# Attention inside a mixture-of-experts kernel: probabilities kept as float32 stationary operands, q and k laid out by the host

## The chip, the cores and the metric

The kernel runs on one core of one Trainium2 chip. The metric is the device time of one execution in microseconds (us). The engines are named as the profile names them: PE is TensorE (matrix products; PEld is its loading of the stationary operand), DVE is VectorE, ACT is ScalarE, POOL is GpSimd, SP issues DMAs. A matrix product holds one operand in the array (stationary, loaded first) and streams the other past it (moving).

## What is computed

Three stages: attention on queries that are averaged in pairs, a dense layer pair with a softmax gate and layer norm, and eight experts of which each token takes one. Only the first stage and the host's part are touched.

```python
B, H, S, D = 4, 8, 1152, 64
q_pool = q.reshape(B, H, S // 2, 2, D).mean(axis=3)
scores = (1.0 / np.sqrt(D)) * np.matmul(q_pool, k.transpose(0, 1, 3, 2))
scores = scores - np.max(scores, axis=-1, keepdims=True)
attn = np.exp(scores)
attn = attn / (np.sum(attn, axis=-1, keepdims=True) + 1e-09)
attn_out = np.matmul(attn, v)
...
x = attn_out.transpose(0, 2, 1, 3).reshape(B * S // 2, H * D)
```

## The kernel before

`attention` (line 95) works through 32 heads of 576 pooled queries and 1152 keys. A head is cut into 9 **units**; a unit holds two of the 18 pairs (half of the queries, chunk of 128 keys). float32r is a type of which TensorE takes fewer bits than float32 has, so a float32 value is carried as two float32r parts, high and low.

- `scores` (L267): per unit four products of 288 columns into one `pair` of PSUM banks. `k1` holds high and low parts of the keys, `q1` the high part of the queries twice, and `k2`/`q2` the remaining part together with two rows that subtract the row maximum. ACT then takes the exponential of the bank twice: `ph` rounded to float32r (L281) and `e` in float32 (L282). DVE subtracts them to the low part `pl` (`rest`, L286).
- `pv` (L288): two units later, three float32r products per (half, chunk): stationary the 65 columns of `vh` or `vl` (v and a column of ones, which sums the probabilities), moving 288 columns of `ph` or `pl` (L295, L296, L297). The result is transposed, 65 rows by 288 queries. `finish`, `norm` and `scale` divide it by its sum, by way of DRAM.
- `prepass` (L241): the row maximum must be known before the exponential. For a later head, 14 products (12 of 384 columns, 2 of 288) into a ring of two `bank`s, each followed by a reduction on DVE (L255). `shift` (L259) turns the maxima into rows of `q2`.
- q, k arrive in rows; PE turns them (`transposes`, L211, 19 per head, in the free columns of a `pair`) and ACT copies the result out (`evacuate`, L218). POOL splits q, k and v into parts (L150, L154, L163).

The order of every engine is the order in which the Python code emits instructions (`manual_schedule`). It is set by a table of due times in units: head n starts at g = 9 n, and `at(g - 12.6 + 0.68 * i, prepass, n, i)` puts its part of the maximum two heads ahead. In a unit come: four score products, transposes, the two exponentials, then the products of the unit before last with events between them, then the remaining events, then `pl`. The fillers (L62 to L92) convert weights that arrive as two words. The dense layers start after the last head.

## Time and profile before

| what | us |
|---|---|
| median of three runs | 1198.6 (1197.12 to 1201.09) |
| span of the profiled execution | 1196.7 |
| first score product to last score product (32 heads) | 19.0 to 596.9 |
| the rest: dense layers and experts | 597 to 1196.7 |

The page of the profile gives the span of the profiled execution, from its first to its last instruction, and no other time of it; the three runs lie 0.4 to 4.4 us above that span, the median 1.9 us. Over the span PE is busy for 90%, DVE for 86%, ACT for 70%, POOL for 64%. These are averages over stages with different limits: heads fill the first half, dense layers and experts the second.

### The profile page before, as it was taken

The numbers are of one execution on the slowest core, as the hardware profiler recorded it, in microseconds if no ns is written. First come the engines' busy times: TensorE is split into PE (matmuls) and PEld (weight loads), VectorE is DVE, ScalarE is ACT, GpSimd is POOL, SyncE is SP. The second block draws the span as 40 slices with busy tenths as digits, with TensorE's granted clock in tenths as the row PEclk, the third lists the DMA queues.
The fourth block names the chain that finished last, engine by engine and source line by source line (L and its number), as shares of the span: only waits on it lengthen the run. The fifth ranks groups of instructions, "written<-read, shape, count | busy, mean of one in ns | idle before, by whom it ended". The sixth has DMA issues, their size and how long they took to land. (4 is left out here: it accounts for less than half of the span.)

```text
span 1196.7 us, 19933 instructions
## 1 busy us (share of the span) xinstructions
PE 1075.0 (90%) x6359; PEld 943.0 (79%) x6359; DVE 1029.4 (86%) x1604; ACT 839.4 (70%) x1637; POOL 760.3 (64%) x844
## 2 busy tenths in 40 slices
PE   7999998999999999999998999979726999999996
PEld 6889888888888888888877777767624888888885
DVE  7898888988899999999758788887999898999983
ACT  5787777877788888878844644444634788888883
POOL 7888888888888888898566676665775221111211
PEclk8999999999999999999998999998878899999998
DMA  5344334344444444443120000004352789533700
GB/s 150 94 107 128 107 106 113 101 118 113 114 114 113 123 114 116 119 114 96 54 85 19 27 18 18 18 18 168 105 176 79 233 285 335 165 114 99 258 18 19
DMA packets 73866, 133.83 MB, mean 112 GB/s; under 512 B 22044, under 2 KB 24092, under 8 KB 73632
## 3 DMA queue, kind: packets, MB, share of 16 engines
q1 hardware_dynamic: 69936, 122.79, 33.9%
q0 software_dynamic: 3680, 9.45, 2.2%
q8 instruction: 52, 0.85, 0.3%
q14 instruction: 54, 0.44, 0.1%
q10 hardware_dynamic: 144, 0.29, 0.1%
HBM read 146.02 MB, written 10.82 MB: 131 GB/s over the span
## 5 line engine op out<-in xcount | busy, mean ns | idle before, releaser
L286 DVE TENSOR_TENSOR pl<-e,ph 128x576 fp32r<-128x576 f32 x288 | 286.5, 995 | 17.5 <-ACT e L282 16.4
L255 DVE TENSOR_REDUCE m<-bank 128x1 f32<-128x384 f32 (+1 forms) x435 | 218.2, 528 | 42.7 <-PE bank L254 38.3
L272 PE MATMUL pair<-q,k 128*128 128x288 f32 x1152 | 205.6, 302 | 0.1
L281 ACT ACTIVATE ph<-pair 128x576 fp32r<-128x576 f32 x288 | 190.8, 662 | 3.0 <-PE pair L272 2.8
L282 ACT ACTIVATE e<-pair 128x576 f32<-128x576 f32 x288 | 190.9, 663 | 0.0
L272 PEld LDWEIGHTS pair<-q,k 128*128 128x128 f32 x1152 | 181.2, 193 | 0.5 <-ACT q L224 0.4
L295 PE MATMUL acc<-ph,vh 128*65 128x288 f32 x576 | 179.1, 311 | 0.0
L297 PE MATMUL acc<-pl,vh 128*65 128x288 f32 x576 | 172.5, 299 | 1.0 <-DVE pl L286 0.8
L296 PE MATMUL acc<-ph,vl 128*65 128x288 f32 x576 | 172.2, 299 | 0.0
L970 POOL DMA_INDIRECT out_y<-x,rows x23 | 25.2, 1095 | 202.0 <-ACT x L969 197.4
L254 PE MATMUL bank<-k,q 128*128 128x384 f32 (+1 forms) x435 | 140.8, 345 | 11.9 <-DVE m L255 10.6
L855 DVE SCALAR_TENSOR_TENSOR junk<-x,en 128x512 f32<-128x512 f32 x99 | 145.9, 1474 | 2.4
L756 PE MATMUL acc<-wo_hi,lh 128*128 128x512 f32 x264 | 109.2, 414 | 14.2 <-ACT lh L868 14.2
L756 PE MATMUL pair<-wi_hi,xl 128*128 128x512 f32 x268 | 106.7, 398 | 5.6 <-DVE xl L931 5.6
L756 PE MATMUL pair<-wi_hi,xh 128*128 128x512 f32 x268 | 109.0, 407 | 0.0
L756 PE MATMUL acc<-wo_hi,ll 128*128 128x512 f32 x264 | 107.1, 406 | 0.4 <-DVE ll L869 0.4
L756 PE MATMUL acc<-wo_lo,lh 128*128 128x512 f32 x264 | 106.1, 402 | 1.2 <-DVE wo_lo L781 1.2
L756 PE MATMUL pair<-wi_lo,xh 128*128 128x512 f32 x268 | 105.8, 395 | 0.0
L254 PEld LDWEIGHTS bank<-k,q 128*128 128x128 f32 (+1 forms) x435 | 79.7, 191 | 20.3 <-DVE m L255 18.8
L224 ACT CAST q<-pair 128x256 fp32r<-128x256 f32 x128 | 48.1, 376 | 60.2 <-PE pair L214 60.2
L869 DVE TENSOR_TENSOR ll<-bank,lh 128x512 fp32r<-128x512 f32 x82 | 52.7, 684 | 40.7 <-ACT lh L868 39.7
L296 PEld LDWEIGHTS acc<-ph,vl 128*65 128x65 f32 x576 | 80.4, 140 | 5.3
(216 smaller groups left out, 2653.2 us busy)
## 6 DMA issues: line engine op xcount, KB each, us to landing
raw<-in_moe_w SPq DMA_DIRECT2D x184, 512.0 KB
vn<-in_v SPq DMA_DIRECT2D x32, 288.0 KB
k<-k SPq DMA_DIRECT2D x32, 288.0 KB
kn<-in_k SPq DMA_DIRECT2D x31, 288.0 KB
k<-k SPq DMA_DIRECT2D x62, 144.0 KB
qn<-in_q SPq DMA_DIRECT2D x32, 256.0 KB
rb<-rd SPq DMA_DIRECT2D x32, 144.0 KB
xT<-xu SPq DMA_DIRECT2D x32, 144.0 KB
```

What stands on the lines that cost most here:

```text
L254: nc.tensor.matmul(out=pp[:p, :w], lhsT=lhsT, rhs=rhs[:, u * w:(u + 1) * w])
L255: nc.vector.tensor_reduce(out=m3[:p, t, u:u + 1], in_=pp[:p, :w], axis=AX.X, op=ALU.max)
L272: nc.tensor.matmul(out=ps[:, i, :QH], lhsT=d[f"k{j}"][:, ch * P:(ch + 1) * P], rhs=d[f"q{j}"][:, hf * QH:(hf + 1) * QH], start=(j == 1), s ...
L281: nc.scalar.activation(out=ph, in_=sv, func=AF.Exp, scale=SC)
L282: nc.scalar.activation(out=e, in_=sv, func=AF.Exp, scale=SC)
L286: nc.vector.tensor_tensor(out=pl, in0=e, in1=ph.bitcast(F32), op=ALU.subtract)
L295: nc.tensor.matmul(out=acc, lhsT=vh, rhs=ph[:, i], start=(ch == 0), stop=False)
L296: nc.tensor.matmul(out=acc, lhsT=d["vl"][:, ch, 0:D + 1], rhs=ph[:, i], start=False, stop=False)
L297: nc.tensor.matmul(out=acc, lhsT=vh, rhs=pl[:, i], start=False, stop=(ch == KC - 1))
L756: nc.tensor.matmul(out=out, lhsT=lhsT, rhs=rhs, start=first and id(out) not in outs[:i], stop=last and id(out) not in outs[i + 1:])
L855: nc.vector.scalar_tensor_tensor(out=self.junk("v", DM), in0=x2, scalar=1.0, in1=en, op0=ALU.mult, op1=ALU.mult, accum_out=to)
L869: nc.vector.tensor_tensor(out=hl[:, o], in0=pt, in1=hh[:, o].bitcast(F32), op=ALU.subtract)
```

## The change

- **Exponentials.** `scores` makes one exponential per unit, `e` in float32, into a ring of four buffers with 640 columns, of which the last 64 are zero. `ph`, `pl` and `rest` are gone. A unit is now one chunk of keys for all 576 queries.
- **Products with v.** `pv` has five float32 products per unit: stationary a block of 128 columns of `e`, moving the 66 columns of `v` (64, a column of ones, a column of zeros), all five into one bank. The result stands in rows of queries, so `norm` divides it on DVE straight from PSUM, without DRAM; after each second head `turned` transposes it with five products and two copies on ACT. v is loaded straight into place and no longer split.
- **q and k.** The host stores them transposed. The on-chip transposes (19 per head), their copies on ACT and `dup_q3`/`dup_k3` are gone. Two heads share the tiles `qn`, `kn`, `kl`, `qs`, one in the upper and one in the lower 64 rows. `split_q` and `split_k` write high parts with ACT, low parts with POOL (DVE for the first two heads), and DMAs copy them to the other 64 rows.
- **Row maximum.** 15 products of 384 columns per head, instead of 14. `shift` transposes on DVE and writes the rows of `q2` with four small DMAs.
- **Order of tokens.** It is now the natural one (`rows_of` is gone).

```diff
+        EARLY = ((-14.82, 0.75), (-3.97, 0.55), (4.4, 0.55))
+        vs = [sb.tile([P, KC, D + 2], F32, name=f"v{i}") for i in range(3)]
+        k2s = [sb.tile([P, S], F32R, name=f"k2{i}") for i in range(2)]
+        q1s = [sb.tile([P, QT * P], F32R, name=f"q1{i}") for i in range(4)]
+        q2s = [sb.tile([P, QT * P], F32R, name=f"q2{i}") for i in range(2)]
+        es = [sb.tile([P, QT * P], F32, name=f"e{i}") for i in range(4)]
...
         def load_q(n):
...
+            nc.sync.dma_start(out=shared(n, "qn", [P, 2, NQ])[mine(n)[0]], in_=q[b, h])
...
         def load_k(n):
...
+            (nc.sync if n else nc.scalar).dma_start(out=shared(n, "kn", [P, S])[mine(n)[0]], in_=k[b, h])
...
         def load_v(n):
...
+            st[n]["v"] = t = vs[n % 3]
+            nc.sync.dma_start(out=t[:, :, 0:D], in_=v[b, h].rearrange("(c p) d -> p c d", p=P))
...
         def split_q(n):
...
+            r, o = mine(n)
+            qn, qs = shared(n, "qn", [P, 2, NQ]), shared(n, "qs", [P, NQ], bufs=2)
+            st[n]["q1"] = q1 = q1s[n % 4][:, 0:NQ]
+            (nc.gpsimd if n > 1 else nc.vector).tensor_tensor(out=qs[r], in0=qn[r, 0], in1=qn[r, 1], op=ALU.add)
+            nc.scalar.copy(out=q1[r], in_=qs[r])
+            nc.sync.dma_start(out=q1[o].bitcast(F32), in_=q1[r].bitcast(F32))
...
         def split_q2(n):
...
+            r, o = mine(n)
+            st[n]["q2"] = q2 = q2s[n % 2]
+            nc.gpsimd.tensor_tensor(out=q2[r, 0:NQ], in0=shared(n, "qs", [P, NQ])[r], in1=st[n]["q1"][r].bitcast(F32),
+                                    op=ALU.subtract)
...
         def split_k(n):
...
+            r, o = mine(n)
+            kn, kl = shared(n, "kn", [P, S]), shared(n, "kl", [P, S], F32R)
+            st[n]["k1"] = k1 = sb.tile([P, S], F32R, tag="k1", name="k1", bufs=4)
+            nc.scalar.copy(out=k1[r], in_=kn[r])
+            (nc.gpsimd if n > 1 else nc.vector).tensor_tensor(out=kl[r], in0=kn[r], in1=k1[r].bitcast(F32),
+                                                              op=ALU.subtract)
+            nc.sync.dma_start(out=k1[o].bitcast(F32), in_=kl[r].bitcast(F32))
...
         def dup_k(n):
...
+            r, o = mine(n)
+            st[n]["k2"] = k2 = k2s[n % 2]
+            nc.sync.dma_start(out=k2[r].bitcast(F32), in_=st[n]["k1"][r].bitcast(F32))
...
         def prepass(n, i):
...
+            u, t = divmod(i, QT)
+            w = S // 3
             pp = c.acc() if n < 2 and i % 2 else c.bank()
...
+            nc.tensor.matmul(out=pp[:, :w], lhsT=q1s[n % 4][:, block(t)], rhs=st[n]["k1"][:, u * w:(u + 1) * w])
+            nc.vector.tensor_reduce(out=m3s[n % 2][:, t, u:u + 1], in_=pp[:, :w], axis=AX.X, op=ALU.max)
...
         def shift(n):
...
             nc.vector.tensor_reduce(out=nm, in_=m3s[n % 2], axis=AX.X, op=ALU.max, negate=True)
-            t = d["q2n"]
-            high(t[:, :, 0], nm)
-            low(t[:, :, 1], nm, t[:, :, 0])
...
+            nc.vector.tensor_copy(out=t[:, 0:QT], in_=nm)
+            nc.vector.tensor_tensor(out=t[:, QT:2 * QT], in0=nm, in1=t[:, 0:QT].bitcast(F32), op=ALU.subtract)
+            nc.vector.transpose(out=nt, in_=t.bitcast(F32))
+            row = D - n % 2 * D
+            dst = st[n]["q2"][row:row + 2].bitcast(F32).rearrange("a (t x) -> a t x", x=P)
+            for x in range(0, P, 32):
+                nc.sync.dma_start(out=dst[:, :, x:x + 32], in_=nt[x:x + 2 * QT])
...
+        def scores(n, ch):
             d = st[n]
             ps = c.pair()
-            for i, (hf, ch) in enumerate(items):
+            for hf in range(2):
                 for j in (1, 2):
-                    nc.tensor.matmul(out=ps[:, i, :QH], lhsT=d[f"k{j}"][:, ch * P:(ch + 1) * P],
+                    nc.tensor.matmul(out=ps[:, hf, :QH], lhsT=d[f"k{j}"][:, ch * P:(ch + 1) * P],
                                      rhs=d[f"q{j}"][:, hf * QH:(hf + 1) * QH], start=(j == 1), stop=(j == 2))
...
-            ph = sb.tile([P, 2, QH], F32R, tag="ph", name="ph", bufs=3)
-            pl = sb.tile([P, 2, QH], F32R, tag="pl", name="pl", bufs=3)
...
-            sv = ps[:, :, :QH]
-            nc.scalar.activation(out=ph, in_=sv, func=AF.Exp, scale=SC)
-            nc.scalar.activation(out=e, in_=sv, func=AF.Exp, scale=SC)
-            return ph, pl, e
...
-        def rest(ph, pl, e):
-            nc.vector.tensor_tensor(out=pl, in0=e, in1=ph.bitcast(F32), op=ALU.subtract)
...
-        def pv(n, items, ph, pl, i):
+            e = es[(n * KC + ch) % 4]
+            nc.scalar.activation(out=e[:, 0:NQ].rearrange("p (a b) -> p a b", a=2), in_=ps[:, :, :QH], func=AF.Exp, scale=SC)
+            return e
...
+        def pv(n, ch, e, t):
...
-                vh = d["vh"][:, ch, 0:D + 1]
-                nc.tensor.matmul(out=acc, lhsT=vh, rhs=ph[:, i], start=(ch == 0), stop=False)
-                nc.tensor.matmul(out=acc, lhsT=d["vl"][:, ch, 0:D + 1], rhs=ph[:, i], start=False, stop=False)
-                nc.tensor.matmul(out=acc, lhsT=vh, rhs=pl[:, i], start=False, stop=(ch == KC - 1))
...
+            if ch == t == 0:
+                d["acc"] = c.acc()[:, 0:QT * (D + 2)].rearrange("p (t x) -> p t x", t=QT)
+            nc.tensor.matmul(out=d["acc"][:, t], lhsT=e[:, block(t)], rhs=d["v"][:, ch],
+                             start=(ch == 0 and t == 0), stop=(ch == KC - 1 and t == QT - 1), skip_group_check=True)
...
         def norm(n):
+            acc, d = st[n]["acc"], st[n - n % 2]
+            rz = xn.tile([P, QT], F32, tag="rz", name="rz", bufs=2)
+            nc.vector.tensor_scalar(out=rz, in0=acc[:, :, D], scalar1=EPS, scalar2=None, op0=ALU.add)
+            nc.vector.reciprocal(out=rz, in_=rz)
+            if n % 2 == 0:
+                d["xq"] = xn.tile([P, QT, P], F32, tag="xq", name="xq", bufs=2)
+            nc.vector.tensor_tensor(out=d["xq"][:, :, mine(n)[0]], in0=acc[:, :, 0:D],
+                                    in1=rz[:, :, None].to_broadcast([P, QT, D]), op=ALU.mult)
+        def turned(n):
...
+            xq = st[n - 1]["xq"]
+            xu = xn.tile([P, NQ], F32, tag="xu", name="xu", bufs=2)
+            for lo, hi in ((0, QT - 1), (QT - 1, QT)):
+                pt = c.bank().rearrange("p (a b) -> p a b", b=P)
+                for t in range(lo, hi):
+                    nc.tensor.transpose(pt[:, t - lo], xq[:, t], c.idf)
+                if lo == 0:
+                    nc.scalar.copy(out=xu[:, 0:4 * P].rearrange("p (a b) -> p a b", b=P), in_=pt)
+                else:
+                    nc.scalar.copy(out=xu[:, 4 * P:], in_=pt[:, 0, 0:D])
+            nc.sync.dma_start(out=xT[:, h // 2, b * NQ:(b + 1) * NQ].bitcast(F32), in_=xu)
             st[n].clear()
...
+            at(g - 31, load_k, n)
+            at(g - 30.5, load_q, n)
+            at(g - 15, load_v, n)
+            at(g - 26, split_q, n)
+            at(g - 25, split_k, n)
+            at(g - 8, split_q2, n)
+            at(g - 8.5, dup_k, n)
+            for i in range(3 * QT):
+                at(EARLY[n][0] + EARLY[n][1] * i if n < 3 else g - 13.2 + 0.6 * i, prepass, n, i)
+            at(g - 3.6, shift, n)
             for i, f in enumerate(filler(n)):
                 at(g + (-3, 1, 2, 3)[i], f)
...
+            at(g + 11, norm, n)
+            if n % 2:
+                at(g + 12.5, turned, n)
...
-                time = n * NU + u
-                job = jobs.get(time)
-                ph, pl, e = scores(n, items, job and job[0](*job[1:]))
...
+            for ch in range(KC):
+                e = scores(n, ch)
+                todo = due(n * KC + ch + 1)
...
-                for i in range(2):
-                    if todo:
+                for t in range(QT):
+                    if todo and t in (0, 2):
                         todo.pop(0)()
                     if old:
-                        pv(*old, i)
+                        pv(*old, t)
...
-        for blk in range(2 * NTT):
-            base, step = rows_of(blk)
-            r = (blk % 2) * D
-            iota(None, None, [[0, 1]], base=base + 1, mult=step, out=row[r:r + D, blk // 2:blk // 2 + 1])
+        iota(None, None, [[P, NTT]], base=1, mult=1, out=row)
...
-        a = np.ascontiguousarray(inputs[name])
+        a = np.asarray(inputs[name])
+        if name == "q":
+            a = a.reshape(B, H, NQ, 2, D).transpose(0, 1, 4, 3, 2)
+        elif name == "k":
+            a = a.transpose(0, 1, 3, 2)
+        a = np.ascontiguousarray(a)
         if a.dtype == np.float64:
```

PE, about half way through the heads. Before: one unit. `q`, `k` are the score operands, `idr`/`khl` a transpose, `ph`, `pl`, `vh`, `vl` the products with v, `bank` the row maximum.

```order
L272 MATMUL pair<-q_4119,k_4185 128x288
L272 MATMUL pair<-q_4641,k_130 128x288
L272 MATMUL pair<-q_4119,k_4185 128x288
L272 MATMUL pair<-q_4641,k_130 128x288
L214 MATMUL pair<-idr,khl 128x128 x2
L295 MATMUL acc<-ph,vh_126 65x288
L296 MATMUL acc<-ph,vl_135 65x288
L297 MATMUL acc<-pl,vh_126 65x288
L254 MATMUL bank<-k_4476,q_4410 128x384
L295 MATMUL acc<-ph,vh_126 65x288
L296 MATMUL acc<-ph,vl_135 65x288
L297 MATMUL acc<-pl,vh_126 65x288
```

PE in the changed kernel, one unit at about the same place; `v`, `e` are the float32 products.

```order
L214 MATMUL pair<-q_134,k_2697 128x288
L214 MATMUL pair<-q_136,k_130 128x288
L214 MATMUL pair<-q_134,k_2697 128x288
L214 MATMUL pair<-q_136,k_130 128x288
L192 MATMUL bank<-k_2900,q_131 128x384
L224 MATMUL acc<-v_126,e_138 128x66 x2
L192 MATMUL bank<-k_3087,q_132 128x384
L224 MATMUL acc<-v_126,e_138 128x66 x3
```

The scores and the row maximum stand as before; six products of 288 columns and two transposes became five of 66 columns.

DVE, before: about three units. `m` is a part of the row maximum, `pl` the low part, `raw` a filler, `dc` the sums of the probabilities.

```order
L286 TENSOR_TENSOR pl<-e,ph 128x576
L67 TENSOR_SCALAR a<-raw 128x256
L69 SCALAR_TENSOR_TENSOR a<-raw,a 128x256
L71 TENSOR_SCALAR m<-raw 128x256
L255 TENSOR_REDUCE m_133<-bank 128x1 x2
L286 TENSOR_TENSOR pl<-e,ph 128x576
L255 TENSOR_REDUCE m_133<-bank 128x1
L286 TENSOR_TENSOR pl<-e,ph 128x576
```

DVE in the changed kernel: most of one head. `rz`, `xq` are the division, `nm`, `nt` the rows that subtract the maximum.

```order
L193 TENSOR_REDUCE m_142<-bank 128x1 x2
L230 TENSOR_SCALAR rz<-acc 128x5
L231 RECIPROCAL rz<-rz 128x5
L234 TENSOR_TENSOR xq<-acc,rz 128x5x64
L193 TENSOR_REDUCE m_142<-bank 128x1 x4
L193 TENSOR_REDUCE m_141<-bank 128x1 x2
L200 TENSOR_REDUCE nm<-m_142 128x5
L201 CAST nm_144<-nm 128x5
L202 TENSOR_TENSOR nm_144<-nm,nm_144 128x5
L203 STREAM_TRANSPOSE nt<-nm_144 128x32
L193 TENSOR_REDUCE m_141<-bank 128x1 x7
L67 TENSOR_SCALAR a<-raw 128x256
```

The subtraction in every unit is gone; the reductions of the maximum stay, and six short instructions per head (division and rows of the maximum) take the place of two (L313, L314).

## Rows read from the trace of the kernel before

**Rows 1.** Busy time by stretch: us, then each engine's busy us (instructions), PE clock.

```profile
300.00:480.70 180.70, 169.43 (x1243) 159.27 (x1242) 168.89 (x292) 146.17 (x333) 156.04 (x193) 0.99 0.42 117
```

**Rows 2.** Instructions by line, 300 to 480.7 us, DVE and ACT: busy us, mean ns | idle.

```profile
L286 DVE TENSOR_TENSOR pl<-e,ph 128x576 fp32r<-128x576 f32 x91 | 95.6, 1050 | 2.8 <-ACT e L282 2.7
L255 DVE TENSOR_REDUCE m<-bank 128x1 f32<-128x384 f32 x121 | 62.3, 541 | 7.3 <-PE bank L254 6.5
L281 ACT ACTIVATE ph<-pair 128x576 fp32r<-128x576 f32 x91 | 60.3, 662 | 0.0
L69 DVE SCALAR_TENSOR_TENSOR a<-raw,a 128x256 int32<-128x256 int32 x10 | 4.3, 425 | 0.3
L79 ACT ACTIVATE s<-raw 128x256 f32<-128x256 int32 x10 | 4.5, 453 | 0.0
L313 DVE TENSOR_SCALAR dc<-dc 64x9 f32<-64x9 f32 x10 | 5.6, 559 | 1.3 <-DMA dc<-xu 1.3
```

**Rows 3.** Waits, 300 to 480.7 us: us in total, times, longest.

```profile
PEld bank L254 <- DVE m L255: 7.6, 11, 0.9
PE pair L214 <- POOL q2n L154: 6.6, 7, 2.0
```

**Rows 4.** PE in order of time, about two units: start us, length us.

```profile
300.64 0.70 PE L272 MATMUL pair<-q,k 128*128 128x288 f32 x4
301.18 0.28 PE L214 MATMUL pair<-idr,q1n 128*128 128x128 f32 x2
301.30 0.31 PE L295 MATMUL acc<-ph,vh 128*65 128x288 f32 x1
...
302.11 0.34 PE L254 MATMUL bank<-k,q 128*128 128x384 f32 x1
302.28 0.69 PE L272 MATMUL pair<-q,k 128*128 128x288 f32 x4
```

**Rows 5.** Short products with 128 stationary columns, in order of time.

```profile
829.66 1.42 PEld L699 LDWEIGHTS bank<-bb,xT 128*128 128x128 f32 x12 [2.42 <-DVE ll L869]
829.66 1.51 PE L699 MATMUL bank<-bb,xT 128*128 128x20 f32 x12 [1.99 <-DVE ll L869]
...
760.55 1.03 PE L866 MATMUL bank<-idf,ln 128*128 128x128 f32 x8
```

**Rows 6.** One line's instructions: ns min/median/max, first and last start us.

```profile
L699 PEld LDWEIGHTS bank<-bb,xT x12: 186/192/193, 829.7 to 830.9; 128*128 128x128 f32 x12
L866 PE MATMUL bank<-idf,ln x328: 270/272/475, 613.1 to 1178.3; 128*128 128x128 f32 x164
L866 PEld LDWEIGHTS bank<-idf,ln x328: 137/140/230, 613.1 to 1178.2; 128*128 128x128 f32 x164
L214 PEld LDWEIGHTS pair<-idr,khl x288: 137/140/223, 6.9 to 564.4; 128*128 128x128 f32 x144
L272 PE MATMUL pair<-q,k x1152: 289/296/445, 19.0 to 596.9; 128*128 128x288 f32 x192
```

**Rows 7.** Instructions by line, 300 to 480.7 us, POOL.

```profile
L323 POOL TENSOR_TENSOR xu<-xu,rb 64x576 f32<-64x576 f32 x10 | 18.9, 1893 | 0.0
L154 POOL TENSOR_TENSOR khl<-kn,khl 128x576 fp32r<-128x576 f32 x10 | 15.0, 1499 | 0.8
L87 POOL TENSOR_TENSOR z<-a,z 128x256 f32<-128x256 f32 x10 | 11.9, 1192 | 0.8
L81 POOL TENSOR_SCALAR z<-m 128x256 f32<-128x256 int32 x10 | 8.5, 847 | 16.9 <-DVE m L71 16.9
```

**Rows 8.** Start of the program, and SP's issues of one line, in order of time.

```profile
0.80 0.41 SPq L131 DMA_DIRECT2D qn<-in_q  x1
...
4.80 0.55 DVE L163 TENSOR_TENSOR qs<-qn 128x256 f32<-128x256 f32 x2 [1.76 <-DMA qn<-in_q]
...
8.46 0.69 PE L254 MATMUL bank<-k,q 128*128 128x384 f32 x1 [0.46 <-ACT k L224]
...
307.96 0.55 SPq L257 DMA_DIRECT2D m<-m  x1
```

252 lines of the change are left out of this document (41 added, 211 removed).

## The prediction, made before the run

> **What bounds the kernel now.** I read the heads first, since nothing else changes. From the first to the last score product they take 596.9 - 19.0 = 577.9 us [rows 6], 18.06 us for each of 32 heads. What ends a head? Busy time by stretch [rows 1] has PE at 169.4 and DVE at 168.9 of 180.7 us over ten heads, but the two mean different things. A PE product counts with its pipeline, so the true pace must come from the starts in order of time [rows 4]: four scores from 300.64 to 301.18 are 0.135 us each, six products with v from 301.30 to 302.11 also 0.135, one part of the row maximum 302.11 to 302.28 is 0.17, a transpose (301.18 to 301.30 for two) 0.06. A head then costs PE 36 x 0.135 + 54 x 0.135 + 14 x 0.17 + 19 x 0.06 = 4.86 + 7.29 + 2.38 + 1.14 = 15.7 us, 87% of the head. DVE stands at 93%, more than half of it `pl` [rows 2], and PE is seen to wait for DVE's reductions and for POOL's splits [rows 3]. So DVE, and close behind PE, ACT and POOL, set the 18.06 us; four engines are nearly full at once.
>
> **The change, part by part.**
>
> *DVE, ACT, POOL.* DVE loses nine `pl` of 1.05 us per head [rows 2]. What stays: 15 reductions of 0.541 = 8.1 us, fillers of about 1.0 (three like L69, 0.28 to 0.43), and about 1.9 for nine short instructions (the longest by the nearest row, 0.56 [rows 2]): 11 us. ACT loses nine exponentials of 0.662 [rows 2] and the copies of transposes; nine exponentials (6.0), copies of q and k (576 and 1152 columns, by the same row 0.66 and 1.3), two fillers like L79 (0.9) and the copies of `turned`, 0.4 by the columns, make 9.3 us. POOL: sum and low part of q at 64 x 576, 1.89 each, low part of k at twice that, 3.8, by the nearest row, `xu` [rows 7]; with fillers of 0.85 and 1.19 [rows 7], a third of about 0.7 and a last step or two (0.5 to 1.8), 10.9 to 12.1 us. By `khl`, 1.5 us for 576 elements, it would be less. All three fall far below 18 us, so none of these savings is gained as such: they only hand the bound to PE.
>
> *PE.* Scores stay, 4.86 us. The transposes go (-1.14). The row maximum is 15 x 0.17 = 2.55. `turned` adds 2.5 float32 transposes per head at (1.03 - 0.272) / 7 = 0.108 us [rows 5, 6], 0.27 us. What decides is the 45 float32 products with v, which replace 54 at 0.135: above 7.29 / 45 = 0.162 us each they cost PE more than before. The trace has no float32 product outside transposes. Its bounds:
>
> - From below: each product loads 128 new columns of `e`. Twelve short products with new 128-column loads run (1.42 - 0.192) / 11 = 0.112 us apart at the full clock [rows 5, 6], although only 20 columns stream. The load is the pace, and shortening the stream to 66 columns gains nothing beyond it: 0.112 us, 5.0 us per head.
> - From above: a float32 value has two parts, so a product has four partial ones; if each brings its own load, 4 x 0.112 = 0.448 us, 20.2 us per head.
> - Taken: 2 x 0.112 = 0.224 us. A float32 transpose takes 0.108 us against 0.06 for a float32r one [rows 4, 5], so the moving side of a float32 operand runs as two parts within one instruction. I take the stationary side to be two parts too, and these must be loaded one after the other; the streams, 2 x 66 columns at 0.108 / 128 each, are 0.056 us and lie behind the next load. 45 x 0.224 = 10.1 us.
>
> Sum for PE: 4.86 + 2.55 + 10.08 + 0.27 = 17.76 us per head against 18.06 now: -0.30 x 32 = **-9.6 us**. PE takes the bound from DVE and gives back nearly all that the others gain.
>
> On the two-part reading the Trainium skill, "FP8 and Floating Point Precision", section "TensorE Precision Notes", says that true FP32 takes four passes through the array. It doesn't say how many loads they need: with two, the sum above stands, with four, the upper bound.
>
> *Waits that are added.* `nt` must reach `q2` before the head's first score. It is due 3.6 units before, 7.1 us. Its four issues take some 0.55 us each on SP [rows 8], the landing at most 4.0 (the first load of q: issued 0.80, used 4.80 [rows 8]): 6.2 us, hidden by 0.9. Ahead of it on SP stands the copy of `kl`, which waits for POOL's sum, filler and low part, 1.89 + 0.85 + 3.8 = 6.5 us after a due time 3.4 units (6.7 us) earlier; behind that copy wait v, `xT`, kn and `nt`. Both just fit; without the cover, a us per head is 32 us. ACT's copy of q waits for POOL's sum, up to 1.9 us, with exponentials queued behind it; PE wants an exponential two units (3.9 us) after its scores, so that is covered. `norm` and `turned` come a unit after the work that they need. DVE has 7 us spare per head, so the wait of PE for reductions (0.76 us a head now, [rows 3]) should shrink.
>
> *Start and end.* Now the first part of the row maximum starts at 8.46, 3.7 us after q is there [rows 8]. Then two DMA copies stand in that path, and `nt` in the next, each up to 4.0 us, in place of PE transposes with their copies: +1 to +5, taken **+2 us**. The dense stage starts after the last head on products of earlier heads; the sums that went through DRAM were not waited for there: 0. Natural token order changes no count of slots.
>
> The profiled execution: 1196.7 - 9.6 + 2 = 1189.1 us. The median of the runs is 1.9 above its span, so **1191 us**. Own range of this case: with 0.108 per load 17.40 us per head, 1180; with DVE's wait of 0.76 kept, 1215.
>
> **Rivals.**
>
> 1. *One load's worth.* Both parts of `e` come in with one load and the streams hide: 0.112 us. PE 17.76 - 5.04 = 12.7 us, POOL at most 12.1: (18.06 - 12.7) x 32 = 171, so 1030; there 3.6 units are only 5.1 us and `nt` would be 1.1 us late per head, 1065. For it: the load of a float32 transpose is recorded with 0.140 us, as that of a float32r one [rows 6]. Against: that is the transposing form, and the short float32r products pay 0.112 for one part [rows 5].
> 2. *Loads wait for streams (slower).* If the load of a product's second part can't run beside the first part's stream, a product costs 0.112 + 0.112 + 0.056 = 0.28 us, PE 20.3, 1272 us; if neither load hides, 0.336, PE 22.8, 1352. It decides from 0.231 us per product, where PE reaches 18.06. For it: nothing here streams as briefly as it loads. Against: scores at 0.135 us leave no room for an unhidden load of 0.112 beside 288 columns [rows 4]. The Trainium skill, "TensorE: Matmul & The Clock Gate", section "Part 3: Packing small matmuls — row/col tiling", has loads overlap running products only if their row groups differ, which these never do; by it, the 1352 holds. The trace disagrees, with that 0.135.
> 3. *Four loads (slower).* 0.448 us, PE 27.8 us: +313, 1513 us.
>
> **How the numbers follow.** Forecast 0.53, one load 0.24, loads that wait 0.15, four loads 0.08. About 0.3%, 3.6 us, is what a measurement of this kernel can tell from no change: 1195.0 to 1202.2. The forecast's case lies on 1180 to 1215 with its centre at 1191: of its 0.53, 0.33 are faster, 0.13 the same, 0.07 slower. With rival 1: faster 0.57; same 0.13; slower 0.07 + 0.15 + 0.08 = 0.30. The range reaches from rival 1 to the milder half of rival 2: 1035 to 1275 leaves out four loads, the other half of rival 2 and an edge of rival 1, together under 0.2. The case alone would be 1180 to 1215.
>
> **What would show it.** In the changed profile: starts of the `acc<-v,e` products 0.22 us apart where five stand together, with PEld busy without a gap; two loads and two products counted for each (2880, where the program has 1440). DVE near 11 us, ACT 9 and POOL 11 to 12 per head. Scores still 0.135 apart, the head 17.8 us. First score near 21 us. PE idle before a head's first score, released by DMA `nt`, would prove the wait wrong; idle before `bank`, released by DVE, the cover of the reductions. The forecast is wrong if that pace is 0.11 (rival 1) or 0.28 and more (rivals 2 and 3), or if heads are longer than PE's sum.

## The result, and the profile after

The changed kernel takes 1212.4 us (median; 1210.8 to 1216.4) against 1199.6 us (1197.1 to 1201.1) for the kernel before on the same chip. The ratio is 1.012, with a 95% interval of 1.009 to 1.014: **slower by 1.2%**, where 1191 and faster had been forecast. The profiled execution spans 1212.0 us, 15.3 more than the one before. The starts of the score products cut both spans into three parts:

| us | before | after | difference | forecast |
|---|---|---|---|---|
| program start to the first score of the second head | 37.8 | 62.7 | +24.9 | +2 |
| from there to the last score product | 558.9 | 554.9 | -4.0 | -9.3 (31 heads x 0.30) |
| last score product to the end | 599.9 | 594.2 | -5.7 | 0 |

Here, in the table of the experiments, in the raw starts of number 9 and where a first score is named in the text, starts count from a point 0.13 us behind the zero of the profile's rows. Two of the nine runs of kernel 3 below (1219 and 1221 us) were in a slower state of the chip; its time in the table is the median of the other seven, and with these two it is the 1204.4 that the expectations quote.

**The heads.** Busy time by stretch and two groups by line, of the changed kernel, 300 to 480.7 us; columns as in [rows 1, 2]:

```profile
300.00:480.70 180.70, 177.87 (x1436) 176.68 (x1434) 108.70 (x250) 85.96 (x140) 83.80 (x73) 1.00 0.47 114
...
L224 PEld LDWEIGHTS acc<-v,e 128*128 128x128 f32 x899 | 116.7, 191 | 0.0
L192 PEld LDWEIGHTS bank<-k,q 128*128 128x128 f32 x150 | 27.8, 191 | 4.0 <-ACT xu L247 4.0
L175 POOL TENSOR_TENSOR kl<-kn,k 64x1152 fp32r<-64x1152 f32 x10 | 26.4, 2637 | 24.6 <-issue 12.5 <-ACT k L174 12.0
```

Against [rows 1], DVE fell from 168.9 to 108.7 of 180.7 us, ACT from 146.2 to 86.0, POOL from 156.0 to 83.8. TensorE rose from 169.4 to 177.9, and its load side is busy for 176.7: it now bounds the heads alone. Over the whole program the page counts 2880 loads for the 1440 products with v. Two stretches in order of time show the pace and the one wait that is left:

```profile
301.16 0.69 PE L214 MATMUL pair<-q,k 128*128 128x288 f32 x4
301.69 1.22 PE L224 MATMUL acc<-v,e 128*128 128x66 f32 x10
302.76 0.44 PE L192 MATMUL bank<-k,q 128*128 128x384 f32 x1
...
304.82 0.72 PE L245 MATMUL bank<-idf,xq 128*128 128x128 f32 x5
305.46 0.58 ACT L247 COPY xu<-bank 128x512 f32<-128x512 f32 x1 [0.25 <-PE bank L245]
305.94 0.22 ACT L249 COPY xu<-bank 128x64 f32<-128x64 f32 x1
306.10 0.19 PEld L192 LDWEIGHTS bank<-k,q 128*128 128x128 f32 x1 [0.80 <-ACT xu L247]
306.10 0.44 PE L192 MATMUL bank<-k,q 128*128 128x384 f32 x1 [0.56 <-ACT xu L247]
```

Five products are ten instructions, and from 301.69 to 302.76 they take 1.07 to 1.12 us, 0.22 each. In every second head the five transposes of `turned` (L245) take both of the two `bank` tiles. The next part of the row maximum (L192) needs one, and waits 0.8 us until ACT has copied the first (L247). By the starts, even heads (counted from one) take 17.4 us and odd ones 18.75.

**The start.** In order of time, the changed kernel, SP and the engines that it waits for:

```profile
10.61 0.46 SPq L177 DMA_DIRECT2D k<-kl  x1
11.11 0.60 SPq L149 DMA_DIRECT2D kn<-in_k  x1
11.75 0.78 SPq L145 DMA_DIRECT2D qn<-in_q  x1
13.98 0.66 PE L192 MATMUL bank<-k,q 128*128 128x384 f32 x1 [13.98 <-DMA k<-kl]
...
16.52 0.76 DVE L160 TENSOR_TENSOR qs<-qn 64x576 f32<-64x576 f32 x1 [5.94 <-DMA qn<-in_q]
...
20.45 0.56 DVE L193 TENSOR_REDUCE m<-bank 128x1 f32<-128x384 f32 x1
...
21.15 0.66 PE L192 MATMUL bank<-k,q 128*128 128x384 f32 x1 [5.55 <-DVE m L193]
...
28.68 0.21 DVE L203 STREAM_TRANSPOSE nt<-nm 128x32 f32<-128x32 f32 x1
...
32.45 2.60 POOL L175 TENSOR_TENSOR kl<-kn,k 64x1152 fp32r<-64x1152 f32 x1 [1.83 <-ACT k L174]
35.08 0.46 SPq L177 DMA_DIRECT2D k<-kl  x1
...
37.39 2.78 SPq L207 DMA_DIRECT2D q<-nt  x4
...
41.63 1.06 PE L214 MATMUL pair<-q,k 128*128 128x288 f32 x3 [10.38 <-DMA q<-nt]
```

Two queues stand (heads are numbered from 0 here, as in the code). First, SP copies head 0's low part of k at 10.61, after DVE has made it, and only then issues the loads of head 1. DVE has head 1's sum in its queue ahead of head 0's first reduction, so it waits 5.94 us for that load, and PE 5.55 us for DVE. Second, `nt` is ready at 28.9, but SP stands at the copy of head 2's low part of k, which POOL ends at 35.05. The four issues of `nt` go out from 37.39, and PE waits 10.38 us for them. Then the first head runs at half pace. One group by line, first for 41 to 54 us and then for 55 to 68:

```profile
L214 PE MATMUL pair<-q,k 128*128 128x288 f32 x19 | 5.7, 449 | 10.4 <-DMA q<-nt 10.4
...
L214 PE MATMUL pair<-q,k 128*128 128x288 f32 x28 | 5.1, 303 | 0.0
```

The first stretch has 449 ns for one product, the second 303. By their starts they are 0.24 us apart until 52, which is 288 columns at 1.2 GHz, and 0.134 from 55 on, about the higher of the two levels. The clock column of the profile shows 1.00 in both stretches, but the trace's records of the granted clock begin only at 54.7 us, with the rise; ahead of that the starts are the evidence, not the column.

### The profile page after: what moved, and what is told of

Same layout as the page of the kernel before. It is cut to its first block, busy times and chain, and to the rows that moved or that the text cites. A ratio compares the mean times of both kernels' runs of the same rounds, so it can differ in the third digit from the quotient of the medians.

```text
span 1212.0 us, 19715 instructions
## 1 busy us (share of the span) xinstructions
PE 1105.0 (91%) x7014; PEld 997.9 (82%) x7014; DVE 845.0 (70%) x1475; ACT 647.9 (53%) x1022; POOL 536.4 (44%) x501
## 5 line engine op out<-in xcount | busy, mean ns | idle before, releaser
L193 DVE TENSOR_REDUCE m<-bank 128x1 f32<-128x384 f32 x466 | 256.7, 557 | 217.7 <-PE bank L192 205.1
L224 PEld LDWEIGHTS acc<-v,e 128*128 128x128 f32 x2880 | 376.3, 192 | 0.1
L224 PE MATMUL acc<-v,e 128*128 128x66 f32 x2880 | 369.1, 268 | 0.0
L214 PE MATMUL pair<-q,k 128*128 128x288 f32 x1152 | 210.7, 305 | 10.4 <-DMA q<-nt 10.4
L192 PE MATMUL bank<-k,q 128*128 128x384 f32 x466 | 182.8, 403 | 28.3 <-DMA k<-kl 14.0
L645 PE MATMUL acc<-wo_hi,lh 128*128 128x512 f32 x264 | 107.0, 405 | 12.5 <-ACT lh L757 12.5
L192 PEld LDWEIGHTS bank<-k,q 128*128 128x128 f32 x466 | 88.5, 195 | 34.2 <-issue 20.6
L175 POOL TENSOR_TENSOR kl<-kn,k 64x1152 fp32r<-64x1152 f32 x30 | 79.0, 2633 | 70.1 <-issue 35.4
L167 POOL TENSOR_TENSOR q<-qs,q 64x576 fp32r<-64x576 f32 x32 | 44.9, 1403 | 140.3 <-PE pair L214 140.2
L758 DVE TENSOR_TENSOR ll<-bank,lh 128x512 fp32r<-128x512 f32 x82 | 52.8, 686 | 38.8 <-ACT lh L757 37.8
L797 ACT CAST xT<-raw 128x1024 fp32r<-128x1024 f32 x62 | 62.7, 1062 | 23.3 <-PE acc L645 17.3
L645 PEld LDWEIGHTS acc<-wo_hi,lh 128*128 128x128 f32 x264 | 50.2, 190 | 26.7 <-ACT lh L757 17.5
L801 DVE TENSOR_TENSOR wo_lo<-raw,wo_hi 128x1024 fp32r<-128x1024 f32 (+1 forms) x55 | 64.9, 1230 | 9.0 <-ACT wo_hi L797 9.0
```

The lines of the kernel that those rows point to most:

```text
L167: nc.gpsimd.tensor_tensor(out=q2[r, 0:NQ], in0=shared(n, "qs", [P, NQ])[r], in1=st[n]["q1"][r].bitcast(F32), op=ALU.subtract)
L175: (nc.gpsimd if n > 1 else nc.vector).tensor_tensor(out=kl[r], in0=kn[r], in1=k1[r].bitcast(F32), op=ALU.subtract)
L192: nc.tensor.matmul(out=pp[:, :w], lhsT=q1s[n % 4][:, block(t)], rhs=st[n]["k1"][:, u * w:(u + 1) * w])
L193: nc.vector.tensor_reduce(out=m3s[n % 2][:, t, u:u + 1], in_=pp[:, :w], axis=AX.X, op=ALU.max)
L214: nc.tensor.matmul(out=ps[:, hf, :QH], lhsT=d[f"k{j}"][:, ch * P:(ch + 1) * P], rhs=d[f"q{j}"][:, hf * QH:(hf + 1) * QH], start=(j == 1), ...
L224: nc.tensor.matmul(out=d["acc"][:, t], lhsT=e[:, block(t)], rhs=d["v"][:, ch], start=(ch == 0 and t == 0), stop=(ch == KC - 1 and t == QT ...
```

## The experiments

All times are medians beside the kernel before on the same chip. "Second head" is the start of its first score product in the trace, "heads" the mean of the later ones. The last three columns are of one profiled run for each kernel, which need not be a typical one: that of number 5 was the fastest of its ten, 3 us below the median, that of number 4 the slowest of its four.

| kernel | us | ratio to before (95%) | second head | heads | last score to end |
|---|---|---|---|---|---|
| before | 1199.6 | | 37.8 | 18.22 | 599.9 |
| changed | 1212.4 | 1.0094 to 1.0141 | 62.7 | 18.04 | 594.2 |
| 1 splits later | 1209.7 | 1.0068 to 1.0112 | 58.1 | 18.07 | 598.1 |
| 2 loads earlier | 1207.3 | 1.0062 to 1.0095 | 53.0 | 18.07 | 598.2 |
| 3 both | 1203.5 | 1.0030 to 1.0064 | 53.4 | 18.04 | 596.2 |
| 4 both, zeros | 1218.3 | 1.0098 to 1.0177 | 57.0 | 18.50 | 597.4 |
| 5 both, weights first | 1199.4 | 1.0001 to 1.0022 | 45.7 | 18.05 | 593.6 |
| 6 as 5, zeros | 1199.6 | 1.0002 to 1.0037 | 45.2 | 18.07 | 598.0 |
| 7 pair, two steps | 1216.9 | 1.0144 to 1.0178 | 59.0 | 18.09 | 599.6 |
| 8 pair, one step | 1202.2 | 1.0020 to 1.0050 | 59.1 | 17.63 | 598.6 |
| 9 64 columns | 1264.3 | 1.0541 to 1.0576 | 60.5 | 19.67 | 596.3 |
| 10 66 columns | 1187.9 | 0.9898 to 0.9937 | 57.4 | 17.22 | 595.1 |
| 11 rounded | 1196.6 | one run | 54.9 | 17.73 | 597.9 |
| 12 v stationary | 1359.2 | 1.1326 to 1.1373 | 36.0 | 23.53 | 600.4 |
| 13 the same, mended | 1180.2 | one run | 37.3 | 17.61 | 600.0 |
| 14 = 3 + 8 + 10 | 1175.1 | 0.9776 to 0.9809 | 52.5 | 17.07 | 597.2 |
| 15 = 4 + 8 + 10 | 1175.0 | 0.9779 to 0.9826 | 54.4 | 17.00 | 597.4 |
| 16 = 6 + 8 + 10 | 1170.5 | 0.9732 to 0.9793 | 45.5 | 17.02 | 600.2 |

**The start: 1, 2 and 3.** Number 1 puts head 2's splits behind `shift` of head 0 on the queues, number 2 head 1's loads ahead of head 0's copies, number 3 does both.

```diff
-            at(g - 31, load_k, n)
-            at(g - 30.5, load_q, n)
+            at(-30 if n == 1 else g - 31, load_k, n)
+            at(-29.5 if n == 1 else g - 30.5, load_q, n)
...
-            at(g - 26, split_q, n)
-            at(g - 25, split_k, n)
+            at(-3.55 if n == 2 else g - 26, split_q, n)
+            at(-3.5 if n == 2 else g - 25, split_k, n)
```

> The changed kernel with one reordering at the start: the splits of head 2 are put behind the rows of the maximum of head 0, so that the four small DMAs of nt no longer stand behind the copy of kl of head 2 on SP. Theory (the start lost 24.9 us by that queue and by DVE's wait for head 1's load): PE's idle 10.4 us before the second score product falls to 2 to 4 us, the second head starts 7 to 9 us earlier, total about 1204. Rival (the start is paid back later, since work that waits there would have to be done anyway): head 0 becomes longer by as much, total 1212, no change.

> The changed kernel with the loads of head 1 issued right behind those of head 0, ahead of the copies that wait on SP. Theory: DVE does the sum of head 1 without its 5.9 us wait, the gap of PE from 15.1 to 21.1 closes, the rows of the maximum of head 0 are there some 5 us earlier, and everything behind moves by 5 to 10 us: total 1202 to 1207. Rival (the copy of kl of head 2 sets nt anyway): 1 to 2 us, total about 1211.

> The changed kernel with both reorderings of the start: loads of head 1 early, splits of head 2 behind the rows of the maximum of head 0. Alone they brought the start of head 1 from 62.7 us to 58.1 and 53.0. Theory (two separate links of one chain): they add up, the first score comes near 25 us and head 1 begins at 46 to 49, 14 to 17 us earlier than in the changed kernel; total 1196 to 1201, the rest of the program differing by some us with the half-clock stretches. Rival (both remove the same wait): head 1 at 53, total 1207.

What PE waits for until 60 us, first in number 2 and then in number 3 (us in total, times, longest):

```profile
PE bank L192 <- DMA k<-kl: 13.7, 1, 13.7
PE pair L214 <- DMA q<-nt: 10.4, 1, 10.4
...
PE pair L214 <- DMA q<-nt: 2.0, 1, 2.0
```

Number 2 takes away the 5.5 us behind DVE; the wait for `nt` remains, and goes with number 1's edit. Both hazards are real: number 1 brings the second head 4.6 us forward, less than the 7 to 9 expected, and number 2 9.7. But together they don't add up: the second head begins at 53.4 in number 3 and at 53.0 in number 2. In number 3 the first head starts to run 8 us earlier, and its scores stay 0.24 us apart until 49; in number 2 they are 0.134 apart from 41 on. The same ten microseconds, 40 to 50 us, in number 3 and then in number 5, which follows:

```profile
40.00:50.00 10.00, 10.00 (x45) 10.00 (x45) 3.56 (x9) 1.36 (x3) 4.19 (x5) 1.00 0.62 137
...
40.00:50.00 10.00, 10.00 (x83) 10.00 (x82) 6.34 (x13) 3.92 (x6) 3.89 (x4) 1.00 0.67 160
```

PE counts as busy throughout in both, with 45 instructions in one and 83 in the other.

**The first head: 4, 5 and 6.** Is it held by the clock, or by something that keeps it there? Number 4 adds products of zeros to number 3 while PE has nothing to do.

```diff
+        def warm(count):
+            pp = c.pair()
+            for i in range(count):
+                nc.tensor.matmul(out=pp[:, 0, :S // 3], lhsT=wz[:, 0:P], rhs=wz)
...
+        warm(36)
-        for f in due(0):
+        for i, f in enumerate(due(0)):
             f()
+            if events_pre[i]:
+                warm(1)
+        warm(8)
```

> The same products of zeros in the kernel that has only the loads and splits of the first heads in the other order (1204.4; its second head began at 53.4 us, and score products were 0.24 us apart until 49). Theory: scores 0.134 apart from the first head on, the second head at 45 to 48, 1196 to 1200. Rival: no difference, 1203 to 1207.

It came out slower, with both theories missed. Busy time by stretch, number 4; then PE at its longest standstill in number 4 and in number 14, which follows below:

```profile
28.00:34.00 6.00, 6.00 (x40) 6.00 (x38) 1.02 (x2) 1.30 (x2) 2.07 (x2) 0.81 0.70 179
34.00:40.00 6.00, 2.71 (x15) 2.58 (x14) 3.34 (x8) 3.75 (x6) 2.70 (x3) 0.76 0.27 64
40.00:60.00 20.00, 20.00 (x89) 20.00 (x87) 6.73 (x14) 4.01 (x7) 7.55 (x7) 0.50 0.39 88
60.00:80.00 20.00, 20.00 (x89) 20.00 (x89) 6.01 (x17) 5.97 (x10) 6.02 (x6) 0.50 0.30 72
...
38.08 0.69 PE L200 MATMUL acc<-k,q 128*128 128x384 f32 x1 [3.29 <-DVE m L201]
...
38.41 0.69 PE L195 MATMUL acc<-k,q 128*128 128x384 f32 x1 [3.85 <-DVE m L196]
```

The scores did start at 0.13 us apart from 30 on. Then PE stood for 3.3 us behind DVE, the granted clock fell to 0.50 at 37, and it stayed there until 85 although PE was busy without a gap. DVE had stood because its queue held the conversion of a weight (L67) whose load SP issued late. That wait is in number 3 as well, 5.3 us long. It comes from my own edit: the splits at -3.5 stand ahead of that load, due at -3. Number 5 puts them behind it (-2.9 and -2.85), number 6 adds the zeros.

> Loads of the second head early as before, and the split of the third head behind the first load of MoE weights on SP's queue (at -2.9 instead of -3.55), so that this load is issued at about 26.7 instead of 30.5 us and VectorE does not wait 5 us for it in the first head. No products of zeros. Theory: the first head is set by the clock, half pace until 45 to 50 us, and VectorE's wait was hidden behind it: 1200 to 1205, as with the other order (1204.4). Rival: the wait of VectorE is what held the first head: second head at 46 to 48 and 1196 to 1199.

> The same order with the products of zeros ahead of the first scores. Theory (clock): the engine comes to the first scores at full pace and, since nothing makes it stand for 3 us any more, stays there: scores 0.13 us apart through the first head, second head at 45 to 47, 1194 to 1199. In the earlier kernel with these products the pace fell back at 37 us, behind a standstill of 3.3 us, and stayed at half until 84. Rival: the pace falls to half in the first head though no standstill is over 1 us: 1203 to 1220, and the standstill was not the cause.

DVE's waits for 20 to 60 us, number 3 and then number 5:

```profile
DVE a L67 <- DMA raw<-in_moe_w_in: 5.3, 1, 5.3
...
DVE a L67 <- DMA raw<-in_moe_w_in: 0.2, 1, 0.2
```

In number 5 the second head begins at 45.7 and not at 53.4. With 1199.4 us for the kernel that is close to the rival's figures (46 to 48 and 1196 to 1199), against the theory that I held: the pace was up by 34 us without any zeros, and stayed up. Number 6 keeps full pace from its first scores and needs 17.2 us for the first head against 20.9; but these scores begin 3.2 us later (28.0 for 24.8), among products of zeros, and the end is the same, 1199.6 and 1199.4. So the order of the queues is worth 13.0 us of the changed kernel's time, and filling PE nothing more.

What DVE's wait does once the pace is up, four runs that have it show alike: in numbers 1, 4, 14 and 15 PE stands for 2.6, 3.3, 3.9 and 4.3 us behind DVE, and in that standstill or within 2 us behind it the granted clock falls to 0.50 (at 45, 37, 38 and 38 us); in numbers 5 and 6, where PE never stands for over 1.1 us once the pace is up, it doesn't fall in the first head. Number 3 is not explained by it. There the clock records begin with the rise at 50.4 us, in number 5 at 33.6, though until 37 us PE's products follow one another in number 3 without a gap, as they do in number 5. Why the rise came so late, no row shows, and one profiled run can't tell the order of the queues from chance; by the medians numbers 3 and 5 are 4 us apart, and not the 7.7 of these two traces.

**`turned`: 7 and 8.** The five transposes get the tile of two banks that the scores use, in place of both `bank` tiles. Number 7 copies four out ahead of the fifth; number 8 makes all five first.

```diff
-            for lo, hi in ((0, QT - 1), (QT - 1, QT)):
-                pt = c.bank().rearrange("p (a b) -> p a b", b=P)
-                for t in range(lo, hi):
-                    nc.tensor.transpose(pt[:, t - lo], xq[:, t], c.idf)
+            pt = c.pair().rearrange("p c (a b) -> p (c a) b", b=P)
+            for t in range(QT):
+                nc.tensor.transpose(pt[:, t], xq[:, t], c.idf)
```

> The changed kernel with the five transposes of each second head in a pair of PSUM banks of the scores' ring, not in the ring of two banks of the row maximum. Theory (the next row maximum waits for ACT's copy out of the bank, some 0.8 us for each pair of heads): odd and even heads come closer (17.4 and 18.75 become 17.4 and 17.95), 16 times 0.8 = 13 us, total about 1200. Rival (the extra 1.34 us is the price of the five products themselves and of the switch between kinds of products): no change, 1212; or the wait moves to the scores, which share the ring: 1212 or more.

> As the earlier attempt with a pair of banks of the scores' ring, but all five transposes stand ahead of the two copies (there the fifth waited for the copy of the first four, since both banks are one tile). Theory (the 1.35 us by which every second head is longer are 0.55 of products and 0.75 of waiting for ACT's copy out of the ring of two banks): heads of 17.4 and 18.0, total about 1200. Rival (the scores now wait for ACT's copies, or the price is the switch itself): 18.75 stays, 1212.

PE's waits in the heads of the changed kernel, then of number 7:

```profile
PE bank L192 <- ACT xu L247: 8.5, 15, 0.6
...
PE pair L246 <- ACT xu L248: 10.1, 15, 0.7
```

Number 7 only moved the wait: its fifth transpose stands for ACT's copy out of the tile that it shares. In number 8 PE has no such wait, odd heads fall from 18.76 to 17.92 and the kernel by 10 us. A transposed pair then costs 0.5 us, five times 0.1.

**The price of a load: 9, 10 and 11.** The fifth block of queries holds 64. Numbers 9 and 10 make its product with 64 and with 66 stationary columns in place of 128; number 11 gives v and the exponentials the rounded type (`F32R`), with POOL rounding v.

```diff
-            nc.tensor.matmul(out=d["acc"][:, t], lhsT=e[:, block(t)], rhs=d["v"][:, ch],
+            p = P if t < QT - 1 else D + 2
+            nc.tensor.matmul(out=d["acc"][:p, t], lhsT=e[:, t * P:t * P + p], rhs=d["v"][:, ch],
```

> The changed kernel with a stationary operand of 64 columns, not 128, for the last 64 queries (the fifth product of each unit); the division is done in two parts for it. The same 66 columns are streamed by the same number of products. Theory (two loads of 128 columns, 0.111 us each, are the pace): the fifth product falls from 0.223 to about 0.12 us, 9 x 0.1 per head, the head from 18.08 to about 17.2, total 1183. Rival (a fixed price per float32 product, or its stream, is the pace): no change at 1212, or some us more for DVE's extra instructions.

> The changed kernel with a stationary operand of 66 columns for the last 64 queries. With 64 columns the fifth product's two parts did come 0.055 us after each other, but PE stood still for 0.15 us before and after them, and the head grew by 1.6 us. Theory (loads are the pace, and the standstill belongs to operands of at most 64 columns, for which the array is set up otherwise): no standstill, 0.9 us less per head, 17.2, total about 1183. Rival (any change of the stationary operand's width costs the standstill): 19.7 us per head again, 1264.

> Exponentials and v in the rounded type instead of float32, the rest as in the kernel of the change: the low parts of both are left out. Theory of two loads for each product: the product becomes one instruction with one load, 0.112 us apart instead of 0.223, the head loses 45 x 0.1115 = 5.0 us where nothing else ends last; ACT needs some 10 us in a head, so heads of 12.8 to 14.5 us and 1212 - 31 x 3.5 to 5 = 1055 to 1105. Rival (the pace of a product is set by something else than the number of loads, such as the eviction or the order of the waits): 1190 to 1215.

Raw starts in number 9, the end of the fourth product, the fifth and the next load (us, ns, instruction, line):

```
302.399 192 LDWEIGHTS 225 acc<-v,e
302.457 275 MATMUL    225 acc<-v,e
302.660 133 LDWEIGHTS 225 acc<-v,e
302.662 272 MATMUL    225 acc<-v,e
302.715 136 LDWEIGHTS 225 acc<-v,e
302.770 222 MATMUL    225 acc<-v,e
302.920 186 LDWEIGHTS 192 bank<-k,q
```

The two loads of 64 columns are 0.055 us apart, half of 0.1115, as a load-bound product wants it. But PE stands for some 0.15 us ahead of them and again behind, and the kernel loses 52 us. With 66 columns the loads are 0.060 apart and nobody stands. The load side of number 10, 300 to 480.7 us, then that of number 11:

```profile
L228 PEld LDWEIGHTS acc<-v,e 128*128 128x128 f32 x756 | 101.4, 191 | 0.0
L228 PEld LDWEIGHTS acc<-v,e 128*66 128x66 f32 x190 | 19.0, 140 | 0.0
...
L228 PEld LDWEIGHTS acc<-v,e 128*128 128x128 f32 x459 | 78.2, 215 | 0.0
```

Number 10 is 0.8% faster than the kernel before. Even heads lose 0.83 us; nine products that are 2 x 0.0515 us shorter make 0.93. In number 11 the count of loads per product is one, and five of them start 0.11 us apart, from 306.17 to 306.61: 0.11 for a product with one load, 0.22 with two. Its shortest heads take 12.5 us, below the range that I gave, and yet the kernel took 1196.6 instead of 1055 to 1105:

```profile
100.00:200.00 100.00, 86.60 (x556) 84.11 (x556) 60.21 (x142) 48.94 (x81) 55.74 (x60) 0.86 0.46 110
...
PE pair L218 <- DMA q<-nt: 28.5, 17, 2.2
PE bank L196 <- DVE m L197: 16.6, 15, 1.7
PE bank L196 <- ACT xu L251: 8.4, 13, 1.3
```

The first line is one stretch, the others PE's waits from 100 to 560 us. Where PE comes down to 12.5 us, the distances that are written out in units shrink with it: `nt` comes late, as rival 1 had it, and the granted clock drops to 0.86 in these stretches (174 us at half in all the heads). The gain of the loads went there.

**One part alone: 12 and 13.** The kernel before with the exponentials once, in float32, and v (65 columns, float32) stationary, with the old layout and its transposes. The last pair of lines is in number 13 alone.

```diff
-            nc.scalar.activation(out=ph, in_=sv, func=AF.Exp, scale=SC)
-            nc.scalar.activation(out=e, in_=sv, func=AF.Exp, scale=SC)
...
-            nc.vector.tensor_tensor(out=pl, in0=e, in1=ph.bitcast(F32), op=ALU.subtract)
+            e = sb.tile([P, 2, QH], F32, tag="e", name="e", bufs=4)
+            nc.scalar.activation(out=e, in_=ps[:, :, :QH], func=AF.Exp, scale=SC)
...
+                nc.tensor.matmul(out=acc, lhsT=d["v"][:, ch, 0:D + 1], rhs=e[:, i], start=(ch == 0), stop=(ch == KC - 1))
...
-            at(g - 17, load_v, n)
+            at(g - 15, load_v, n)
```

> The kernel before with one part of the change alone: exponentials once in float32, and the product with v as one float32 product of 288 columns with v (65 columns) stationary, in place of three float32r ones; q and k, transposes, order and start as before. Theory (loads of one kind hide where streams are long; a float32 product streams four times): 4 x 288 columns at 0.054 us per 128 are 0.486 us, PE 4.86 + 18 x 0.486 + 2.38 + 1.14 = 17.1 us per head, DVE down to 9: head 17.1 to 17.6, total 1168 to 1184, faster than before. Rival (PE's waits for POOL and ACT stay, as POOL and ACT were nearly full too): 18 us per head, 1198.

> One part of the change alone in the kernel before: the exponentials once, in float32, with v (65 columns, float32) stationary and 288 exponentials moving, v loaded two units later than in the first try so that no product waits for it. From the first try's rows: a product is two instructions 0.24 us apart, 0.48 us in all, against three of 0.135 before, 18 of them in a head: +1.35 us on a PE-bound head of 18.0, so heads of 19.0 to 19.5 and 1225 to 1245. Rival (the products were not what the first try's heads of 23.8 us waited on, and ACT's and VectorE's lower load wins back more than the products cost): 1165 to 1195.

Number 12 can't be read for its total: its load of v comes in the program ahead of the last products that read the same buffer, so that these products use another head's v and wait for its load. First the products of number 12 (300 to 480 us), then number 13, busy time by stretch and a part of a unit in order of time:

```profile
L277 PE MATMUL acc<-e,v 128*65 128x288 f32 x267 | 96.8, 463 | 28.9 <-DMA v<-in_v 28.9
...
300.00:480.70 180.70, 180.70 (x1074) 145.37 (x1073) 90.57 (x203) 99.26 (x245) 100.16 (x175) 1.00 0.47 120
...
311.73 0.65 PE L277 MATMUL acc<-e,v 128*65 128x288 f32 x2
312.00 0.55 PE L244 MATMUL bank<-k,q 128*128 128x384 f32 x1
312.39 0.70 PE L262 MATMUL pair<-q,k 128*128 128x288 f32 x4
```

Number 13 took 1180.2 us in one run, 13 us below the fastest of the runs of before beside it (1193.7). That is the rival's range. PE never waits, its granted clock stays at 1.00 in this stretch, and all but the last few heads take 17.7 us. A product with 288 moving columns costs 0.48 us, as I had it, and my total was wrong all the same: I had added 1.35 us to a head of 18.0, but the PE-bound sum of the kernel before was 15.7, the rest being waits. In this one run the part that took work from DVE, ACT and POOL pays by itself. Turning the product round so that the exponentials are stationary costs 45 x 0.223 = 10.0 us in a head, where 18 x 0.48 = 8.6 would do.

**The sum: 14, 15 and 16.** The edits of the start, `turned` and the 66 columns together; 15 and 16 with the zeros, 16 in the order of number 5.

> The four edits that were timed one by one, together: the loads and the splits of the first heads in the other order (alone 1204.4), the five transposes in one pair of banks (1202.2), the 66-column stationary of the fifth product (1187.9); the kernel of the change took 1212.4. If the pieces are separate, as I hold: even heads 16.5, odd heads 17.0 to 17.1 us instead of 17.4 and 18.75, which is 1.28 us x 31 = 40 us, and the second head begins at about 53; 1160 to 1172. Rival: the odd heads of the 66-column kernel (17.95) wait for something that the pair of banks does not give, and only the sum of the smaller parts comes: 1176 to 1184.

> The kernel before this one in the list, with products of zeros (384 columns) on TensorE while it has nothing to do in the start: 36 ahead of the first row-maximum, one behind each row-maximum product ahead of the first scores, 8 more before these. Theory: the first head runs at half pace (score products 0.24 us apart until about 50 us) because the engine has stood for most of the time until then; with the products it comes to the first scores at full pace (0.134) and the second head begins 5 to 8 us earlier: 1154 to 1166, 5 to 8 below its neighbour. Rival: the pace of the first head has nothing to do with what the engine did before: no difference, or up to 3 us more where the products stand in the way.

> All edits together: this start with the products of zeros, the five transposes in one pair of banks, the 66-column stationary. Heads of 17.0 as in the run of the four edits (1175.1, second head at 52.5): second head at 44 to 46 and 1166 to 1170. Rival (the clock's time comes back elsewhere): 1174 to 1178.

Number 14 lies between its two theories: heads of 17.07 where the singles promised 16.75. The waits behind ACT's copies are gone; others take a part of their place (100 to 560 us):

```profile
PEld bank L195 <- DVE m L196: 3.1, 8, 0.8
PEld pair L217 <- POOL q L170: 2.3, 4, 0.7
```

Number 15 gained nothing from the zeros, as number 4; its first head also falls to half pace at 38. Number 16 is the fastest kernel here, 2.4% faster than the kernel before (2.1 to 2.7). The time at its end is 600.2 us, 3 more than in 14, which gives back nearly half of the 7 us that the start gained.

## Why the prediction was wrong, and where it held

*The pace of the products* was right: 0.223 us against 0.224, two loads of 0.1115, 2880 of them, with the streams beneath. The three rivals fall: one load's worth would be 0.112 (measured where the type is rounded, number 11), loads that wait 0.28, four loads 0.448. The Trainium skill, "TensorE: Matmul & The Clock Gate", section "Part 3: Packing small matmuls — row/col tiling", stood behind the second rival; the load side is busy for 176.7 of 180.7 us beside a PE that is busy for 177.9, so here loads run beside products that use all rows: a pace of 0.223 us has room for the two loads and for no stream behind them.

*The relief of DVE, ACT and POOL* was right, with POOL's part over-sized: 10.9, 8.6 and 8.4 us per head against 11, 9.3 and 10.9 to 12.1. POOL's sums cost 1.41 and 2.64 us, less than `xu` at 1.89 had made me assume [rows 7].

*The sum for a PE-bound head* was right without `turned`: 17.49 by the forecast's terms, 17.4 measured. **`turned` was mis-sized**: I counted 0.27 us per head of transposes and no wait. It costs 1.35 for every second head, 0.67 per head, of which 0.8 us is the wait for ACT's copy out of the ring of two; number 8 takes it back. The sentence that failed is "`norm` and `turned` come a unit after the work that they need": it looks at who makes the input, and not at the tiles that the output takes from the next instruction in PE's queue. This is where most of the expected gain of the heads went: -4.0 in place of -9.3.

*The time to beat* was read too coarsely. The 18.06 us are an average of two kinds of head. Two lines of PE in order of time, then busy time by stretch, of the kernel before:

```profile
90.30 0.36 PE L214 MATMUL pair<-idr,q2n 128*128 128x128 f32 x2 [1.98 <-POOL q2n L154]
91.67 1.16 PE L272 MATMUL pair<-q,k 128*128 128x288 f32 x4
...
60.00:320.00 260.00, 237.56 (x1698) 225.17 (x1697) 226.11 (x403) 199.15 (x456) 219.68 (x274) 0.95 0.41 113
320.00:580.00 260.00, 244.92 (x1807) 230.29 (x1807) 246.09 (x430) 212.93 (x482) 221.44 (x271) 1.00 0.40 110
```

Eight times until 317 us PE waits 1.9 to 2.0 us for POOL, and each time the granted clock is then 0.50 for 3.4 us; such a head takes 20.3 us, its neighbour 17.1. From 320 us on the waits stay below 1.0, the clock stays at 1.00, and a head takes 17.65. The prediction's rows of the heads come from 300 us on and show the second kind almost alone. So from the second to the seventeenth head the changed kernel gains 10.3 us (18.08 against 18.72 per head), by having neither the wait nor the half pace, and over the last fifteen it loses 6.3 (18.0 against 17.65): where the kernel before ran undisturbed, the change makes a head longer.

**The start is the step that failed**: +2 forecast, +24.9 measured, enough to turn the sign. I priced the two added copies in the path of the first row maximum and `nt` behind them, 1 to 5 us in all; the first part of the row maximum alone starts 5.5 us later, at 13.98 for 8.46 [rows 8]. I did name the hazard, SP standing at the copy of `kl` with `nt` behind it, and found that "both just fit". In the heads they do: `nt` is not among PE's waits between 60 and 617 us. In the start the distances in units don't hold, since the events of three heads are drawn together there, and the same pair costs 10.4 us; DVE's wait for head 1's load costs 5.5; and the first head then runs at half pace until about 54 us. Number 5 takes 17.1 of the 24.9 back, by four due times. Nearly 8 us remain: the first score at 24.8 instead of 18.8, and a first head of 20.9 instead of 19.0.

*The end.* The same work takes 594.2 us after and 599.9 before. The forecast had 0, and nothing in the change was to shorten it: this part is luck. The clock records have 54.8 us at half after the last score, against 67.8 before. Over all kernels of the table the two go together (51.6 us with 593.6 at one end, 67.8 with 599.9 at the other), broadly and not in order; what decides how much of it there is, no run shows. Without this difference the span would have grown by 21 us.

## What to carry to other kernels

Price a stationary operand by its loads before anything else: a float32 product with 128 new columns costs two of them, 0.22 us, where the stream is short, as with the 66 columns here. When work moves from compute engines to DMA copies, read the in-order queue that issues them once for the steady state and once for the start, where the distances between steps are others; and ask of each moved step which buffer its output takes from its successor. Read the time to beat head by head before you average it. Add a cost to the sum of the engine that bears it, not to the time of the stage, as number 13 shows.

## What the runs showed of the hardware

- A float32 product outside a transpose is two loads and two products. With 128 stationary columns the two are 0.1115 us apart, with 66 columns 0.060, with 65 stationary and 288 moving columns 0.24: the longer of load and stream sets the pace.
- Between operands of 128 and of 64 stationary columns PE stood for about 0.15 us in both directions; with 66 columns it did not.
- The profile's clock column showed 1.00 ahead of the trace's first clock record, which was a rise to full: in the start of the changed kernel 288 columns took 0.24 us until 52 us, and the first record is at 54.7.
- In several runs the granted clock fell to 0.50 in or just behind a standstill of PE: for 3.4 us each time at standstills of 2.0 us in the heads of the kernel before, for 10 us at one of 3.9 us in number 14, and for 48 us at one of 3.3 us in number 4, though PE was busy throughout from 40 us on.
